# Linear attention times a gated block on one core: the last 64 columns of q made with the last third of k and v, tokens as rows, and turned by PE

## The chip, the cores and the metric

One core of a Trainium2 chip runs the whole kernel as one launch. The time is device microseconds from one execution; a kernel is run several times and the median is compared. The engines named below are PE (matrix products), DVE (vector), ACT (scalar functions), POOL (general) and SP, which here only issues transfers.

## The reference

With x of 2048 tokens by 576 and xn its layer norm:

```
q, k, v = split(xn @ wqkv)            # 32 heads of 18 columns
phi(t)  = where(t > 0, t + 1, exp(t)) + 1e-6
kv      = sum over tokens of phi(k) * v,   z = sum over tokens of phi(k)
o       = phi(q) @ kv / (phi(q) @ z + 1e-6)
s       = o @ wo
g       = silu((gelu(xn @ w_gate) * (xn @ w_up)) @ w_down)     # 4608 columns inside
out     = x + s * g
```

All data are 32-bit floats. The products are made in several passes over a high and a low word of each operand, which are added in PSUM.

## The kernel before

**Stages.** The 2048 tokens are 16 tiles of 128, in 4 blocks of 512. First the layer norm and the tiles of k and v run, then attention (q, kv times wo, the division, s), then gate and up (with seven products where eight would be written plainly, the same for down), then the product down with the closing arithmetic. The change lies in the first two.

**Operands.** 576 is cut in two halves of 288, and each half into 128, 128 and 32 rows (the 32 rows three times, for the mixed passes). `center` scales a tile of x, `turn` (L160) transposes it on PE into two banks of 3 x 128 columns, so that the last 128 columns of each bank are free, `place` (L169) writes the high words (ACT) and low words (DVE) into the blocks' operands `xo`, and `save` (L186) keeps the whole values in `xf` and gives the banks back.

**A tile of k and v.** `kv_tile` (L378) runs three series of matmuls, `x_mm(t, 0)`, `(t, 1)` and `(t, 2)`, each of 2 halves x 7 passes (`KV_PASSES`) over 384 columns of the 1152 columns of k and v, tokens as rows. Behind the first series the next tile is turned, behind the second it is placed and saved, `k_post` makes phi of k (two DVE passes, an exponential on ACT, an addition on POOL), `v_post` copies v on ACT. `kv_mm` adds a tile's phi(k) times v to two banks of their own, a tile later. `end` is a list of further steps, run behind the third series and ahead of `v_post(t, 2)`. The weights stay in five buffers `wkv` of six pieces, the sixth piece of each holding a part of the sixth (third, half).

**q.** `q_mm` (L400) makes one group of 128 rows of q for a block of 512 tokens, q's columns as rows, in 14 matmuls of 512 columns, and `phi` (L300) follows it: the first pass on DVE, or on ACT where its last argument is true. There are five groups: four of 126 columns (seven heads) with two more columns each, and the last, which has 64 columns twice. `q_store` stores the groups of blocks 0 and 1 to memory (they are loaded later by `q_load`), `q_hold` keeps those of blocks 2 and 3. Tiles 0 to 7 come first, then ten groups of `q_store` with a list `behind` of side work, one entry behind each, then tiles 8 to 15, then `q_hold` of block 2 and of block 3, five groups each, with their own lists of side work.

**The side work at the places of the change.** `difference` forms sums of blocks in place (DVE); `form` builds one of them as an operand in buffer 12 and sends it to memory (`keep`), so that the next `form` has to wait until the copy has left; `spread` and `scales` work out the statistics of two tiles (DVE, two short ACT passes). After tile 15: `kv_done` masks kv, `kv_wo` multiplies it with wo, `make_sel` (L532) makes 0/1 matrices on POOL, with copies on ACT and POOL, and the buffer of denominators. `den(tb)` multiplies phi(q) with z, takes reciprocals (DVE) and splits them in two words; `scale` spreads them over the rows of q by a matmul and multiplies; `halve` cuts the result into words; `s_mm` makes s.

**Order and buffers.** `pin` keeps each engine's instructions in the order of the program, so a wait holds up all that stands behind it on that engine, and transfers are issued in order on SP. PSUM has six banks that are shared in turn (`bank`) and two of their own. Four buffers `tmp` hold short-lived values, six buffers `gl` others; a big buffer is named by its number.

Of the kernel before, what the change touches and what calls it, by code (L numbers as in the profile page):

```python
# [15 lines left out]
P = 128  # L16
# [16 lines left out]


Q4 = 64
Q2 = NHG * P // 2
LN_EPS = 1e-5
# [14 lines left out]
@with_exitstack  # L52
def block_kernel(ctx, tc, x, xe, wq_d, wkv_d, wo, wgu_d, wd_d, out):
    nc = tc.nc
# [105 lines left out]
    def turn(n, new=bank):  # L160

        xs = xstat[n // 2][:, n % 2]
        tiles = [new(f"xt_{n}_{j}") for j in range(2)]
        xts[n] = [t[:, 0 : 3 * P].rearrange("p (k t) -> p k t", k=3) for t in tiles]
        for j in range(2):
            for k in range(3):
                pin(nc.tensor.transpose(xts[n][j][:, k, :], xs[:, j, k * P : (k + 1) * P], ident))  # L167
# [64 lines left out]

    TW = 2 * D // 3
    KV = [(c, j) for c in range(3) for j in range(2)]
    wkv = [big(4 + i, [P, 6, TW], F32R, f"wkv_{i}") for i in range(5)]

    def kv_part(c, j, i):
        n = KV.index((c, j))
        return wkv[n][:, i, :] if n < 5 else wkv[i][:, 5, :]

    raws = {}

    def load_kv(c, j):
        n = KV.index((c, j))
        if n % 2 == 0:
            raws["kv", n // 2] = big((2, 3, 12)[n // 2], [P, 2, 3, TW], F32, f"rw_{n}")
        raws[c, j] = raws["kv", n // 2][:, n % 2]
        dma(out=raws[c, j], in_=wkv_d[c, j])

    def kv_hi(c, j):  # L250
        n = KV.index((c, j))
        if n < 5:
            act(wkv[n][:, 0:3, :], raws[c, j], AF.Copy)
        else:
            for i in range(3):
                act(kv_part(c, j, i), raws[c, j][:, i, :], AF.Copy)

    def kv_lo(c, j, eng, mixed=(False, True)):

        n, raw, r = KV.index((c, j)), raws[c, j], slice(2 * KR, 3 * KR)  # L260
        if False in mixed:
            if n < 5:
                eng("tensor_sub", wkv[n][:, 3:5, :], raw[:, 0:2, :], wkv[n][:, 0:2, :].bitcast(F32))
# [60 lines left out]
    KV_PASSES = [(0, 0), (1, 1), (3, 0), (4, 1), (0, 3), (1, 4), (2, 2)]  # L324
    pkv, pks, vas, es = {}, {}, {}, {}
# [28 lines left out]
    def v_post(t, c):  # L354

        if c == 1:
            vas[t] = slot([P, NHG, P], F32, f"va_{t}")
            pool("memset", vas[t][:, :, 0:1], 1.0)
        va, src = vas[t], pkv.pop((t, c))
        n = 2 * TW - D  # L360
        if c == 1:
            src = src[:, TW - n : TW]
            act(va[:, 0, 1 : GW + 1], src[:, 0:GW], AF.Copy)
            act(va[:, 1, 1 : n - GW + 1], src[:, GW:n], AF.Copy)
        else:
            a = 2 * GW - n
            act(va[:, 1, n - GW + 1 : GW + 1], src[:, 0:a], AF.Copy)
            act(
                va[:, 2:4, 1 : GW + 1],
                src[:, a : a + 2 * GW].rearrange("p (g j) -> p g j", g=2), AF.Copy,  # L370
            )
            act(va[:, 4, 1 : W4 + 1], src[:, a + 2 * GW : TW], AF.Copy)

    def run(todo, n=None):
        for _ in range(len(todo) if n is None else min(n, len(todo))):
            todo.pop(0)()

    def kv_tile(t, mid_=(), end=()):  # L378

# [16 lines left out]
        v_post(t, 2)  # L396

    ph, ph_d = {}, {}

    def q_mm(tb, gi, o):  # L400
# [3 lines left out]
        for j, nm in enumerate(BS[b]):  # L404
            for wi, xi, rows in PASSES:
# [4 lines left out]
                n += 1  # L410
        phi(o, pq, f"q{tb}_{gi}", tb == 3)

    def q_store(tb, gi):
        if gi == 0:
            ph_d[tb] = dr.tile([P, NHG, TBN], F32, name=f"phd_{tb}")
        o = gl_tile([P, TBN], f"ph_{tb}_{gi}")
        q_mm(tb, gi, o)
        dma(out=ph_d[tb][:, gi, :], in_=o)

    def q_hold(tb, i, after):  # L420
        ph[tb] = big(i, [P, NHG, TBN], F32, f"ph_{tb}")
        for gi in range(NHG):
            q_mm(tb, gi, ph[tb][:, gi, :])
            run(after[gi])

    def q_load(tb, i):
# [105 lines left out]
    def make_sel():  # L532
# [4 lines left out]
        at["rd"] = rd = buf[:, n : n + TBN]  # L537
        one = tmp([H, NHG, P], "self")
        pool("memset", one, 1.0)
        four, last = one[:, 0:4, 0:GW], one[:, 4, :].rearrange("p (r j) -> p r j", r=2)  # L540
        for o, pattern, base in ((four, [[GW, 4], [1, GW]], 0), (last, [[0, 2], [1, Q4]], 4 * GW)):
# [13 lines left out]
            base=1 - H, pattern=[[0, 4], [0, P - GW]], channel_multiplier=1,  # L555
        )
        for i in range(4):
# [5 lines left out]
        pool("memset", rd.bitcast(F32), 0.0)  # L563

    HB = TBN // 4

    def den(tb):

        pd = bank(f"d_{tb}")
        for gi in range(NHG):  # L570
            for i in range(4):
                mm(
                    pd[H * i : H * (i + 1), 0:HB], at["zc"][:, gi, :],
                    ph[tb][:, gi, i * HB : (i + 1) * HB],
                    start=(gi == 0), stop=(gi == NHG - 1),
                )
# [11 lines left out]
    def scale(tb, *gs):  # L588

        for gi in gs:  # L590
            pb = bank(f"b_{tb}_{gi}")
            mm(pb, at["sel"][:, gi, :], at["rd"], start=True, stop=True)
            p = ph[tb][:, gi, :]
            vec("tensor_mul", p, p, pb)

    def halve(tb, *gs):
# [3 lines left out]
        for gi in gs:  # L600
            p = ph[tb][:, gi, :]
            if gi == NHG - 1:
# [475 lines left out]
    x_mm(1, 2)  # L1078
    save(2)
    v_post(0, 2)  # L1080
    center(3)
    v_post(1, 2)
    make_masks()
# [21 lines left out]
    x_next(4)  # L1105
    v_post(2, 2)
    load_q(0)
    for n in range(3, 2 * TT):
# [21 lines left out]
    def form(nm):  # L1130
# [3 lines left out]
        0: [lambda: kv_mm(N0 - 1), lambda: difference(0, 3)],  # L1134
        1: [lambda: spread(N0, 2)],
        2: [lambda: scales(N0), lambda: center(N0)],
        3: [lambda: form("T1")],
        4: [lambda: turn(N0), lambda: place(N0)],
        5: [lambda: center(N0 + 1)],
        6: [lambda: form("T3"), lambda: save(N0)],  # L1140
        7: [lambda: spread(N0 + 2, 2), lambda: scales(N0 + 2)],
        8: [],
        9: [],
    }
    for i in range(2 * NHG):
        q_store(*divmod(i, NHG))
        run(behind[i])
    for n in range(N0, 2 * N0):
        ends = []
        if n < 2 * N0 - 2:  # L1150
            ends.append(lambda n=n: center(n + 2) if n == N0 else x_next(n + 2))
        if n in (N0, N0 + 2):
            ends.append(lambda n=n: form("T2" if n == N0 else "T4"))
        if n == 2 * N0 - 3:
            ends.append(load_wo)
        if n == 2 * N0 - 1:
            ends += [lambda i=i: difference(1, i) for i in range(3)]
        kv_tile(n, end=ends)
        if n in (N0, N0 + 2):
            load_x(n + 4, 2)  # L1160
    q_hold(2, 7, [
        [lambda: kv_mm(2 * N0 - 1), kv_done, lambda: difference(1, 3)],
        [lambda: kv_wo(4)],
        [lambda: kv_wo(0), lambda: kv_wo(1), move_rows],
        [lambda: kv_wo(2), lambda: kv_wo(3)],
        [make_sel],
    ])
# [116 lines left out]
```

## Time and profile before

| | us |
|---|---|
| median of 3 runs (1503.47 to 1503.78) | 1503.70 |
| the profiled execution, its own time | 1503.52 |
| its span, first to last instruction | 1501.8 |
| DVE busy | 1062.2 |
| ACT busy | 557.1 |
| POOL busy | 534.3 |

The span is what the trace shows; the time has some 1.7 us around it. A line of a group says: line, engine, operation, what it writes and reads, its shape, how often; then the time that it was busy, the mean of one in ns; then how long the engine had stood idle just before, and what ended that. All operations go through helpers, so L84 is any ACT pass, L87 any DVE pass, L90 most matmuls, L93 any POOL operation, L96 any transfer; the tiles' names tell them apart. In the timeline a row is start, length, engine, line, operation and count, with the idle time before it in brackets; several instructions of one kind are one row. A row by stage has the stretch, then busy time and count of PE, PEld, DVE, ACT and POOL, then the granted clock of PE, the busy share of the transfer engines, and GB/s.

### The profile page before, as it was taken

Reading aid. Unit: us, or ns where it says so; the run is one execution under the profiler, and the core shown is the slowest. Engines: PE = TensorE matmul, PEld = TensorE weight load, DVE = VectorE, ACT = ScalarE, POOL = GpSimd, SP = SyncE. Lnnn points to the kernel's source line nnn. Section 1 sums busy time; section 2 is a strip of 40 time slices with the busy share of each in tenths; the row PEclk is TensorE's granted clock in tenths of the full one; section 3 lists DMA queues with packets and bytes.
Section 4 is the critical chain, followed back from the end, with each engine's and each line's share of the span. In section 5 each row is a group of like instructions: output and inputs, shape, how many; then the busy total and the mean of one; then the engine's idle time right before and its main releaser. Section 6 shows DMA issues by size and latency. Waiting matters only on the chain.

```text
span 1501.8 us, 22404 instructions
## 1 busy us (share of the span) xinstructions
PE 1491.9 (99%) x8430; PEld 1335.1 (89%) x8430; DVE 1062.2 (71%) x1583; ACT 557.1 (37%) x1016; POOL 534.3 (36%) x491
## 2 busy tenths in 40 slices
PE   8999999999999999999999999999999999999998
PEld 8989979988888888888888888888899999999998
DVE  7477467467887877887877788877785566555775
ACT  5524345432322323322233232232445454444443
POOL 4342240136555445655544655544410020000120
PEclk9999999999999999999999999999999999999999
DMA  5424104454434233443333443423597766786873
GB/s 194 182 88 147 58 2 182 158 199 170 172 137 163 110 134 144 172 165 142 135 117 130 172 172 135 161 107 134 212 341 246 234 209 230 234 280 228 296 247 116
DMA packets 112215, 257.35 MB, mean 171 GB/s; under 512 B 10138, under 2 KB 38682, under 8 KB 110058
## 3 DMA queue, kind: packets, MB, share of 16 engines
q1 hardware_dynamic: 110474, 247.00, 46.0%
q0 software_dynamic: 1632, 8.91, 1.6%
q8 instruction: 66, 1.08, 0.3%
q14 instruction: 43, 0.35, 0.1%
HBM read 157.93 MB, written 97.91 MB: 170 GB/s over the span
## 4 chain that ended last, share of the span: by engine, by line
PE 96%; DVE 2%; ACT 1%; POOL 0%; DMA 0%; issue 0%; SPq 0%; ACTq 0%; DVEq 0%; POOLq 0%
PE bd L906 27%; PE al L700 15%; PE de L700 15%; PE ga L700 15%; PE be L700 8%; PE kv L90 7%; PE q L90 4%; PE s L90 4%; PE kv_a L90 1%; PE xt L167 1%; DMA rw<-in_wkv_dram 0%; PE b L90 0%; PE kw L90 0%; PE d L90 0%; DVE wkv L87 0%
## 5 line engine op out<-in xcount | busy, mean ns | idle before, releaser
L906 PEld LDWEIGHTS bd<-t,s 128*128 128x128 f32 x3024 | 400.9, 188 | 0.1
L906 PE MATMUL bd<-t,s 128*128 128x288 f32 x3024 | 401.0, 295 | 0.0
L87 DVE TENSOR_TENSOR s<-sr,s 128x512 fp32r<-128x512 f32 x252 | 176.7, 741 | 119.7 <-ACT s L84 115.2
L84 ACT ACTIVATE s<-sr 128x512 fp32r<-128x512 f32 x252 | 149.3, 626 | 189.4 <-PE bd L906 129.0
L93 POOL TENSOR_TENSOR hs<-h,h 128x512 f32<-128x512 f32 x68 | 94.7, 1401 | 205.3 <-DVE h L87 202.6
L84 ACT ACTIVATE h<-h 128x512 f32<-128x512 f32 x108 | 67.0, 632 | 244.4 <-POOL sm L93 123.1
L93 POOL TENSOR_TENSOR sx<-sx 128x288 f32<-128x288 f32 x24 | 28.2, 1195 | 322.6 <-DVE sx L87 211.6
L90 PE MATMUL kv<-wkv,xo_B 128*128 128x384 f32 x672 | 125.2, 340 | 1.7 <-POOL wkv L93 0.9
L90 PEld LDWEIGHTS kv<-wkv,xo_B 128*128 128x128 f32 x672 | 115.9, 188 | 3.9 <-POOL wkv L93 1.7
L87 DVE TENSOR_TENSOR wa<-raw,wa 128x256 fp32r<-128x256 f32 x72 | 79.1, 1099 | 50.1 <-ACT wa L84 46.9
L93 POOL TENSOR_TENSOR sm<-raw 128x384 f32<-128x384 f32 x72 | 75.9, 1054 | 105.9 <-DMA raw<-in_wgu_dram 92.3
L87 DVE TENSOR_TENSOR h<-h,u 128x512 f32<-128x512 f32 x108 | 95.7, 886 | 3.7
L84 ACT ACTIVATE wa<-sm 128x1152 fp32r<-128x1152 f32 x36 | 41.8, 1161 | 136.6 <-PE de L700 136.6
L93 POOL TENSOR_TENSOR td<-td 128x288 f32<-128x288 f32 x72 | 72.2, 1003 | 50.0 <-DMA td<-in_wd_dram 45.8
L87 DVE TENSOR_TENSOR wa<-sm,wa 128x768 fp32r<-128x768 f32 x72 | 63.1, 876 | 36.9 <-ACT wa L84 36.0
L87 DVE TENSOR_TENSOR wb<-raw,wb 128x256 fp32r<-128x256 f32 (+1 forms) x108 | 71.8, 665 | 7.3 <-ACT wb L84 5.8
L87 DVE TENSOR_TENSOR wb<-sm,wb 128x256 fp32r<-128x256 f32 x72 | 61.4, 853 | 20.5 <-ACT wb L84 20.0
L84 ACT ACTIVATE u<-al 128x512 f32<-128x512 f32 x72 | 40.8, 592 | 88.3 <-PE al L700 88.3
L90 PE MATMUL q<-xo_B,wq 128*128 128x512 f32 x240 | 64.1, 395 | 0.0
L87 DVE TENSOR_TENSOR u<-u,ga 128x512 f32<-128x512 f32 x72 | 49.3, 686 | 19.9 <-PE ga L700 19.3
L700 PE MATMUL al<-xo_B,wa 128*128 128x512 f32 x252 | 63.0, 389 | 0.0
L700 PE MATMUL be<-xr_T,wa 128*128 128x512 f32 x252 | 63.0, 389 | 0.0
(159 smaller groups left out, 2783.5 us busy)
## 6 DMA issues: line engine op xcount, KB each, us to landing
sr<-hs SPq DMA_DIRECT2D x252, 256.0 KB
hs<-h SPq DMA_DIRECT2D x68, 512.0 KB
raw<-in_wgu_dram SPq DMA_DIRECT2D x36, 768.0 KB
hs<-hs SPq DMA_DIRECT2D x102, 256.0 KB
td<-in_wd_dram SPq DMA_DIRECT2D x18, 576.0 KB
td<-td SPq DMA_DIRECT2D x18, 576.0 KB
tr<-td SPq DMA_DIRECT2D x16, 576.0 KB
tr<-in_wd_dram SPq DMA_DIRECT2D x12, 576.0 KB
```

The source lines that it names most:

```text
L84: pin(nc.scalar.activation(*args, **kw))
L87: pin(getattr(nc.vector, op)(*args, **kw))
L90: pin(nc.tensor.matmul(*args, **kw))
L93: pin(getattr(nc.gpsimd, op)(*args, **kw))
L167: pin(nc.tensor.transpose(xts[n][j][:, k, :], xs[:, j, k * P : (k + 1) * P], ident))
L700: nc.tensor.matmul(o, w[0:rows, wi, :], xop[0:rows, xi, :], start=(start and n == 0), stop=(n == len(PASSES) - 1), skip_group_check=True,)
L906: nc.tensor.matmul(banks[j][:, 0:HALF], hw[n, s][:, a, t * P : (t + 1) * P], w[:, c, g % 4], start=(new and g == 0 and m == 0), stop=(g == ...
```

## The change

The last group of q (64 columns) is no longer a product of its own. Its 64 columns of the weights are joined to the last third of k and v, so the third series of each tile has 448 columns instead of 384. `q_post` makes phi of those 64 columns with tokens as rows and writes it twice side by side; `q_turn` transposes the 128 x 128 result on PE, into the free last 128 columns of the banks of a later tile's `turn` (tile t's in the turn of tile t + 2); `q_keep`, at the end of `place`, copies it on ACT into a block's buffer `ph4`, which is stored for blocks 0 and 1. The last two tiles are turned in a bank of their own by `last_turn`.

```
 W4 = WIDTHS[4]
...
-Q2 = NHG * P // 2
+Q2 = 2 * P
...
             for k in range(3):
                 pin(nc.tensor.transpose(xts[n][j][:, k, :], xs[:, j, k * P : (k + 1) * P], ident))
+        q_turn([t for t in sorted(pqt) if t < n - 1], [(t, 3) for t in tiles])
...
+        q_keep()
...
     TW = 2 * D // 3
+    CW = [TW, TW, TW + Q4]
...
-                    o[:, 0:TW], xo[s][BS[b][j]][:, xi, i * P : (i + 1) * P], kv_part(c, j, wi),
+                    o[:, 0 : CW[c]], xo[s][BS[b][j]][:, xi, i * P : (i + 1) * P], kv_part(c, j, wi),
...
+    def q_post(t):
+
+        w = tmp([P, 4, Q4], f"w_q{t}")
+        src, o, e = pkv[t, 2][:, TW : CW[2]], w[:, 2], w[:, 3]
+        vec("tensor_scalar", e, src, 0.0, None, op0=ALU.min)
+        vec("tensor_scalar", o, src, 0.0, EPS, op0=ALU.max, op1=ALU.add)
+        act(e, e, AF.Exp)
+        for i in range(2):
+            pool("tensor_add", w[:, i], o, e)
+        pqt[t] = w[:, 0:2]
+
+    def q_turn(ts, banks):
+
+        for t, (b, i) in zip(ts, banks):
+            o = b[:, i * P : (i + 1) * P]
+            pin(nc.tensor.transpose(o, pqt.pop(t), ident))
+            pqx[t] = o
+
+    def q_keep():
+        for t in sorted(pqx):
+            tb, i = divmod(t, TT)
+            if i == 0:
+                ph4[tb] = gl_tile([P, TBN], f"ph4_{tb}")
+                if tb < 2:
+                    ph_d[tb] = dr.tile([P, NHG, TBN], F32, name=f"phd_{tb}")
+            act(ph4[tb][:, i * P : (i + 1) * P], pqx.pop(t), AF.Copy)
+            if i == TT - 1 and tb < 2:
+                dma(out=ph_d[tb][:, 4, :], in_=ph4[tb])
...
-    def kv_tile(t, mid_=(), end=()):
+    def kv_tile(t, mid_=(), end=(), after=()):
...
         v_post(t, 2)
+        q_post(t)
+        run(list(after))
...
-        phi(o, pq, f"q{tb}_{gi}", tb == 3)
+        phi(o, pq, f"q{tb}_{gi}", tb % 2 == 1)
...
-        for gi in range(NHG):
+        for gi in range(4):
             q_mm(tb, gi, ph[tb][:, gi, :])
```

In the first two tiles, which are written out by hand, `q_post(0)` stands behind `save(2)` and `q_post(1)` behind `center(3)`. The side work is dealt out again, since eight groups of `q_store` are left of ten, and four of five in each `q_hold`:

```
     behind = {
         0: [lambda: kv_mm(N0 - 1), lambda: difference(0, 3)],
-        1: [lambda: spread(N0, 2)],
-        2: [lambda: scales(N0), lambda: center(N0)],
-        3: [lambda: form("T1")],
+        1: [lambda: spread(N0, 2), lambda: scales(N0)],
+        2: [lambda: center(N0), lambda: form("T1")],
+        3: [lambda: spread(N0 + 2, 2), lambda: scales(N0 + 2)],
         4: [lambda: turn(N0), lambda: place(N0)],
-        5: [lambda: center(N0 + 1)],
-        6: [lambda: form("T3"), lambda: save(N0)],
-        7: [lambda: spread(N0 + 2, 2), lambda: scales(N0 + 2)],
-        8: [],
-        9: [],
+        5: [lambda: center(N0 + 1), lambda: form("T3")],
+        6: [lambda: save(N0)],
+        7: [],
     }
-    for i in range(2 * NHG):
-        q_store(*divmod(i, NHG))
+    for i in range(8):
+        q_store(*divmod(i, 4))
...
-        if n in (N0, N0 + 2):
-            ends.append(lambda n=n: form("T2" if n == N0 else "T4"))
+        after = [lambda n=n: form("T2" if n == N0 else "T4")] if n in (N0, N0 + 2) else []
...
+        if n == 2 * N0 - 2:
+            after.append(make_sel)
         if n == 2 * N0 - 1:
+            after.append(copy_sel)
             ends += [lambda i=i: difference(1, i) for i in range(3)]
-        kv_tile(n, end=ends)
+        kv_tile(n, end=ends, after=after)
...
     q_hold(2, 7, [
-        [lambda: kv_mm(2 * N0 - 1), kv_done, lambda: difference(1, 3)],
+        [lambda: kv_mm(2 * N0 - 1), kv_done, last_turn, lambda: difference(1, 3)],
         [lambda: kv_wo(4)],
         [lambda: kv_wo(0), lambda: kv_wo(1), move_rows],
         [lambda: kv_wo(2), lambda: kv_wo(3)],
-        [make_sel],
     ])
     q_hold(3, 8, [
         [lambda: den(2)],
-        [],
         [lambda: scale(2, 0, 1), lambda: halve(2, 0, 1)],
         [lambda: scale(2, 2, 3), lambda: halve(2, 2, 3)],
         [lambda: scale(2, 4), lambda: halve(2, 4)],
```

`copy_sel` is the last part of `make_sel`, its four copies of the 0/1 matrices; the rest of `make_sel` now runs a tile earlier. The weights reach the kernel as three arrays of k and v instead of one, and q's array has 512 columns instead of 640, so `prep_q` works on pieces of 256 columns instead of 320. In `q_hold(3)` one group now stands between `den(2)` and the first `scale`, where there were two.

More of the change, by code (lines that the diff above doesn't have):

```diff
@@ L52, in block_kernel @@
 @with_exitstack
-def block_kernel(ctx, tc, x, xe, wq_d, wkv_d, wo, wgu_d, wd_d, out):
+def block_kernel(ctx, tc, x, xe, wq_d, wkv0_d, wkv1_d, wkv2_d, wo, wgu_d, wd_d, out):
     nc = tc.nc
@@ L233, in block_kernel, with kv_parts @@
     TW = 2 * D // 3
+    CW = [TW, TW, TW + Q4]
     KV = [(c, j) for c in range(3) for j in range(2)]
-    wkv = [big(4 + i, [P, 6, TW], F32R, f"wkv_{i}") for i in range(5)]
+    wkv_d = [wkv0_d, wkv1_d, wkv2_d]
+    wkv = [big(4 + i, [P, 5 * CW[KV[i][0]] + CW[2]], F32R, f"wkv_{i}") for i in range(5)]
+    def kv_parts(n, i0, i1):
+        w = CW[KV[n][0]]
+        return wkv[n][:, i0 * w : i1 * w].rearrange("p (i f) -> p i f", f=w)
     def kv_part(c, j, i):
         n = KV.index((c, j))
-        return wkv[n][:, i, :] if n < 5 else wkv[i][:, 5, :]
+        if n < 5:
+            return kv_parts(n, i, i + 1)[:, 0]
+        w = 5 * CW[KV[i][0]]
+        return wkv[i][:, w : w + CW[2]]
     raws = {}
@@ L245, in load_kv @@
         if n % 2 == 0:
-            raws["kv", n // 2] = big((2, 3, 12)[n // 2], [P, 2, 3, TW], F32, f"rw_{n}")
+            raws["kv", n // 2] = big((2, 3, 12)[n // 2], [P, 2, 3, CW[c]], F32, f"rw_{n}")
         raws[c, j] = raws["kv", n // 2][:, n % 2]
-        dma(out=raws[c, j], in_=wkv_d[c, j])
+        dma(out=raws[c, j], in_=wkv_d[c][j])
     def kv_hi(c, j):
@@ L252, in kv_hi @@
         if n < 5:
-            act(wkv[n][:, 0:3, :], raws[c, j], AF.Copy)
+            act(kv_parts(n, 0, 3), raws[c, j], AF.Copy)
         else:
@@ L262, in kv_lo @@
             if n < 5:
-                eng("tensor_sub", wkv[n][:, 3:5, :], raw[:, 0:2, :], wkv[n][:, 0:2, :].bitcast(F32))
+                eng("tensor_sub", kv_parts(n, 3, 5), raw[:, 0:2, :], kv_parts(n, 0, 2).bitcast(F32))
             else:
@@ L324, in block_kernel @@
     KV_PASSES = [(0, 0), (1, 1), (3, 0), (4, 1), (0, 3), (1, 4), (2, 2)]
-    pkv, pks, vas, es = {}, {}, {}, {}
+    pkv, pks, vas, es, pqt, pqx, ph4, ph, ph_d = ({} for _ in range(9))
     def x_mm(t, c):
@@ L358, in v_post @@
             pool("memset", vas[t][:, :, 0:1], 1.0)
-        va, src = vas[t], pkv.pop((t, c))
+        va, src = vas[t], pkv[t, c]
         n = 2 * TW - D
@@ L396, in kv_tile @@
         v_post(t, 2)
-    ph, ph_d = {}, {}
+        q_post(t)
+        run(list(after))
     def q_mm(tb, gi, o):
@@ L420, in q_hold, with ph_of @@
     def q_hold(tb, i, after):
-        ph[tb] = big(i, [P, NHG, TBN], F32, f"ph_{tb}")
-        for gi in range(NHG):
+        ph[tb] = big(i, [P, 4, TBN], F32, f"ph_{tb}")
+        for gi in range(4):
             q_mm(tb, gi, ph[tb][:, gi, :])
             run(after[gi])
+    def ph_of(tb, gi):
+        return ph4[tb] if gi == 4 and tb > 1 else ph[tb][:, gi, :]
     def q_load(tb, i):
@@ L537, in make_sel @@
         at["rd"] = rd = buf[:, n : n + TBN]
-        one = tmp([H, NHG, P], "self")
+        at["one"] = one = tmp([H, NHG, P], "self")
         pool("memset", one, 1.0)
@@ L556, in make_sel, with copy_sel @@
         )
+        pool("memset", rd.bitcast(F32), 0.0)
+    def copy_sel():
+        one, sel = at["one"], at["sel"]
         for i in range(4):
@@ L592, in scale @@
             mm(pb, at["sel"][:, gi, :], at["rd"], start=True, stop=True)
-            p = ph[tb][:, gi, :]
+            p = ph_of(tb, gi)
             vec("tensor_mul", p, p, pb)
@@ L600, in halve @@
         for gi in gs:
-            p = ph[tb][:, gi, :]
+            p = ph_of(tb, gi)
             if gi == NHG - 1:
@@ L1079, in block_kernel @@
     save(2)
+    q_post(0)
     v_post(0, 2)
     center(3)
+    q_post(1)
     v_post(1, 2)
@@ L1106, in block_kernel @@
     v_post(2, 2)
+    q_post(2)
     load_q(0)
@@ L1251 @@
     xe = np.concatenate([xh] + 3 * [xh[:, :, 2 * P :]], axis=2)
-    wq = np.zeros((D, NHG, P), A_wqkv.dtype)
-    for g in range(4):
-        wq[:, g, 0:GW] = A_wqkv[:, g * GW : (g + 1) * GW]
-        wq[:, g, GW:P] = A_wqkv[:, 4 * GW + Q4 + 2 * g : 4 * GW + Q4 + 2 * g + 2]
-    wq[:, 4, 0:Q4] = wq[:, 4, Q4:P] = A_wqkv[:, 4 * GW : 4 * GW + Q4]
-    wq = halves(wq.reshape(D, NHG * P)).reshape(2, P, 3, 2, Q2).transpose(3, 0, 1, 2, 4)
-    wkv = halves(A_wqkv[:, D:]).reshape(2, P, 3, 3, 2 * D // 3).transpose(3, 0, 1, 2, 4)
+    q, n = A_wqkv[:, 0:D], 2 * D // 3
+    last = q[:, 4 * GW : 4 * GW + Q4]
+    wq = np.concatenate([
+        q[:, i : i + w] for g in range(4)
+        for i, w in ((g * GW, GW), (4 * GW + Q4 + 2 * g, 2))
+    ], axis=1)
+    wq = halves(wq).reshape(2, P, 3, 2, Q2).transpose(3, 0, 1, 2, 4)
+    wkv = [halves(A_wqkv[:, D + c * n : D + (c + 1) * n]) for c in range(2)]
+    wkv.append(halves(np.concatenate([A_wqkv[:, D + 2 * n :], last], axis=1)))
     wgu = np.stack([
@@ L1269 @@
     for name, a in (
-        ("x", xs), ("xe", xe), ("wq", wq), ("wkv", wkv), ("wo", A_wo), ("wgu", wgu), ("wd", wd)
+        ("x", xs), ("xe", xe), ("wq", wq), ("wkv0", wkv[0]),
+        ("wkv1", wkv[1]), ("wkv2", wkv[2]), ("wo", A_wo), ("wgu", wgu), ("wd", wd)
     ):
```

9 lines of the change are left out of this document (5 added, 4 removed).

## The prediction

> **What bounds the kernel now.** I read the page first, then the chain of waits, then the busy time by stage, then PE's own waits, then the timeline at each place that the change touches.
>
> ```profile
> span 1501.8 us, 22404 instructions
> ...
> PE 1491.9 (99%) x8430; PEld 1335.1 (89%) x8430; DVE 1062.2 (71%) x1583; ACT 557.1 (37%) x1016; POOL 534.3 (36%) x491
> ...
> PEclk9999999999999999999999999999999999999999
> ...
> PE 96%; DVE 2%; ACT 1%; POOL 0%; DMA 0%; issue 0%; SPq 0%; ACTq 0%; DVEq 0%; POOLq 0%
> ```
>
> PE is busy at the full granted clock and carries 96% of the chain that ends last, so a matmul taken away is worth its time unless a wait replaces it. The change lies in the first 232 us. Cut at its stages (columns: stretch, length, then busy time of PE, PEld, DVE, ACT, POOL):
>
> ```profile
> 0.00:32.45 32.45, 28.00 (x155) 24.96 (x156) 23.80 (x56) 17.52 (x40) 15.15 (x25) 1.00 0.48 182
> 32.45:82.94 50.49, 50.49 (x324) 50.36 (x323) 26.08 (x69) 22.98 (x64) 19.84 (x23) 1.00 0.45 165
> 82.94:116.54 33.60, 33.60 (x157) 27.99 (x157) 28.13 (x50) 10.43 (x18) 12.45 (x10) 1.00 0.35 141
> 116.54:187.19 70.65, 70.65 (x450) 70.42 (x449) 40.48 (x96) 30.19 (x84) 17.84 (x23) 1.00 0.25 86
> 187.19:209.25 22.06, 22.06 (x103) 17.86 (x101) 17.86 (x31) 7.35 (x18) 6.07 (x7) 1.00 0.01 3
> 209.25:232.42 23.17, 22.65 (x147) 18.51 (x149) 13.29 (x23) 12.44 (x23) 12.15 (x15) 1.00 0.00 1
> ```
>
> These are the start, the tiles of k and v, the first q stage (ten groups), the later tiles, the third token block's q with kv times wo, and the last block's q. PE is full in all but the start and the last stage. DVE has 5.5 us to spare in the first q stage (28.13 of 33.60) and 4.2 in the fifth. PE's waits before 330 us confirm that little is lost:
>
> ```profile
> PE kv L90 <- POOL wkv L93: 0.9, 1, 0.9
> PE b L90 <- DVE aux L87: 0.6, 2, 0.5
> PE kv L90 <- ACT xo_B L84: 0.5, 2, 0.3
> ```
>
> **The change, part by part.** The pace of a matmul is not its mean duration, since neighbours overlap; I take it from runs of them in the chain (start, length, count):
>
> ```profile
> 41.49 4.88 PE kv L90 x28
> ...
> 87.19 12.78 PE q L90 x56
> 99.97 0.66 PE xt L167 x6
> ...
> 277.82 18.65 PE s L90 x140
> ```
>
> Removed: group 4 of q for four token blocks, 4 x 14 = 56 matmuls of 512 columns. The row of q is exactly 56 of them: **-12.78 us**.
>
> Widened: the last third of k and v goes from 384 to 448 columns, in 16 tiles x 14 = 224 matmuls. No row has 448 columns. The paces are 18.65/140 = 0.1332 us at 288, 4.88/28 = 0.1743 at 384, 12.78/56 = 0.2282 at 512: 0.43 and 0.42 ns a column, so 64 columns cost 0.0270 to 0.0274 us and all 224 cost 6.04 to 6.14. The outer bounds are nothing (384's pace) and 12.1 (512's); the three widths lie on a line, so I take **+6.10**.
>
> Added on PE: 16 transposes of 128 x 128, the same operation as in the row of six: 0.66/6 = 0.11 us each, **+1.76**. They write the free last quarter of banks that are held already, and but for the last two they stand behind six others.
>
> ```profile
> L167 PE MATMUL xt<-ident,x 128*128 128x128 f32 x96 | 13.2, 273 | 0.9 <-PE idle L1021 0.8
> ```
>
> This row has 273 ns as the duration of one. [...] Here six take 0.66 us together, so the measurement decides for 0.11 unless they stand alone.
>
> The side work of each tile: two DVE passes of 128x64 from PSUM, one exponential, two POOL adds and one ACT copy of 128x128.
>
> ```profile
> L87 DVE TENSOR_SCALAR e_k<-kv 128x384 f32<-128x384 f32 x16 | 8.9, 558 | 39.3 <-PE kv L90 39.3
> ...
> L87 DVE TENSOR_SCALAR e_k<-kv 128x192 f32<-128x192 f32 x16 | 5.7, 357 | 10.0 <-PE kv L90 9.9
> ...
> L84 ACT ACTIVATE va<-kv 128x60 f32<-128x60 f32 x16 | 3.5, 221 | 9.4 <-PE kv L90 9.4
> L93 POOL TENSOR_TENSOR wq_l<-rq,wq 128x320 fp32r<-128x320 f32 x4 | 3.5, 878 | 0.0
> ```
>
> From 192 and 384 columns a 64-column DVE pass is an estimated 0.22 us (bounds 0 and 0.36); the exponential 0.22; a POOL add 0.3 (bounds 0 and 0.88). Per tile that is 0.44 on DVE, some 0.5 on ACT, 0.6 on POOL, beside DVE 40.48, ACT 30.19 and POOL 17.84 busy of 70.65 us: hidden, if the columns are ready when PE turns them. The turn stands in PE's queue before the next tile's second matmul series, so everything on PE waits for a late add. The worst ordinary tile is one where statistics run on DVE first:
>
> ```profile
> 56.87 0.68 DVE L87 TENSOR_SCALAR x<-x,mv,st 128x768 f32<-128x768 f32 x1
> ```
>
> and in the chain of waits
>
> ```profile
> 58.95 0.65 PE xt L167 x6
> ```
>
> DVE is free at 57.55, so its passes end at 58.0, the exponential at 58.2, the adds at 58.8 (60.0 at their bound). PE reaches the turn at 58.95 + 0.65 + 0.38 (the wider series before it, 6.10/16) = 60.0. Cost nothing; without that cover, each microsecond of lateness costs one, in up to 14 tiles. The extra store of 256 KB per early block goes onto SP once a block, ahead of loads that are wanted tiles later: nothing.
>
> The start: two pieces of the weights are a sixth wider on the last third, so one ACT pass, one DVE pass, POOL's three and a 32-row piece grow, and two tiles' q work comes in.
>
> ```profile
> L84 ACT ACTIVATE wkv<-rw 128x1152 fp32r<-128x1152 f32 x5 | 5.7, 1159 | 0.3 <-DMA rw<-in_wkv_dram 0.3
> ...
> L87 DVE TENSOR_TENSOR wkv<-rw,wkv 128x768 fp32r<-128x768 f32 x3 | 2.9, 954 | 0.0
> ```
>
> ```profile
> 12.00:14.00 2.00, 1.69 (x10) 0.89 (x8) 1.70 (x3) 1.63 (x4) 1.17 (x2) 1.00 1.03 418
> ```
>
> ACT +0.19 and DVE +0.16 by a sixth, four DVE passes 0.9, and 197 KB more at 418 GB/s (the last figure of the stage row, transfers full) 0.5 us. PE comes 0.76 us later itself through two wider series (counted above), which hides most: bounds 0 and 1.8, all in a row; I take **+0.3**, the growth of the two passes ahead of that series.
>
> The last turn: tokens of tiles 14 and 15 are turned behind the first q group of block 2 and kv's last products. Tile 15's DVE passes wait behind three differences.
>
> ```profile
> 184.44 6.44 DVE L87 TENSOR_TENSOR xf_B<-xf_B,xf_B 128x1536 f32<-128x1536 f32 x3
> ...
> 191.15 0.29 PE L90 MATMUL kv_b<-pk,va 128*73 128x72 f32 x2
> ```
>
> DVE 190.88 + 0.44, ACT 0.22, POOL 0.6: 192.15. PE is there at 191.44 + 0.38 = 191.82. Stall 0.3, bounds 0 and 1.5 (adds at 0.88); nearer the first, **+0.4**. Behind it wait block 2's other groups; DVE and ACT have slack there.
>
> The last q stage loses two groups of 3.2 us, under which masks were made and denominators worked out.
>
> ```profile
> 212.29 1.30 PE L90 MATMUL d<-ph,small 128*32 128x128 f32 x40
> ...
> 214.75 1.48 ACT L84 ACTIVATE aux<-self 32x640 fp32r<-32x640 f32 x2 [4.10 <-POOL self L93]
> ...
> 217.50 0.28 DVE L87 TENSOR_SCALAR r<-d 128x128 f32<-128x128 f32 x1
> ...
> 219.20 1.28 DVE L87 TENSOR_TENSOR aux<-r,aux 32x128 fp32r<-32x128 f32 x4 [0.44 <-ACT aux L84]
> ...
> 220.63 0.70 PE L90 MATMUL b<-aux 128*128 128x512 f32 x2 [0.47 <-DVE aux L87]
> ```
>
> Before, the products d end at 213.6, but the reciprocals begin at 217.5, since ACT stands 4.1 us at the mask copies that POOL delays, and DVE behind ACT. The reciprocal chain itself takes 220.48 - 217.50 = 3.0 us. With the masks made a tile earlier it can begin when d ends, and one group of 3.2 us covers it instead of two. The wait of 0.47 should go; the spacing of scaling and group after that is as before. I take **-0.4**, bounds -0.75 (with the 0.28 of the next row, before the last products of s) and +3.2 (a rival).
>
> ```profile
> 231.63 0.56 PEld L90 LDWEIGHTS s<-kv,pq 128*128 128x128 f32 x4 [0.28 <-DVE pq L87]
> ```
>
> The first q stage loses 6.4 us of PE cover as well, and DVE two groups' passes, and the first pass of block 1's four groups goes to ACT.
>
> ```profile
> L87 DVE TENSOR_SCALAR e_q<-q 128x512 f32<-128x512 f32 x15 | 10.3, 687 | 3.6 <-PE q L90 3.5
> ```
>
> By the stage's row DVE needs 28.13 - 8 passes of 0.69 = 22.6 of 27.4 us (33.60 - 6.4 + 0.22): as full as before, so nothing; if it runs over, PE's six banks hold some three groups of backlog.
>
> **Sum:** -12.78 + 6.10 + 1.76 + 0.3 + 0.4 - 0.4 = **-4.6 us**. The span goes from 1501.8 to 1497.2. The profiled execution took 1503.52 us, 1.7 around its span: 1498.9. The median of the runs is 0.18 above it, so **1499.1**.
>
> **Rivals.**
> *The last q stage is DVE's and ACT's.* From d to the first scaling before took 7 us, and half the cover goes. For it: the chain of waits there runs through ACT and DVE. Against: 4.1 us of that was the masks. Price: that one group's cover, 3.2 us: 1502.3.
>
> *Transposes count singly,* 273 ns by the row above: 16 x 0.163 = 2.6 more, 1501.7. [...] For it: two stand alone at the end. Against: 0.66 for six.
>
> *The gain doesn't arrive*, because 448 columns are paced like 512: 6.0 more, 1505.1. Against it: three widths on a line. Break-even is (12.78 - 1.76)/224 = 0.0492 us per matmul above the 384 pace; the line gives 0.0272.
>
> *Slower: the copies of the sums in the first q stage.* One buffer serves both T1 and T3, so the second's build on ACT waits until the first has left for memory.
>
> ```profile
> 101.90 0.32 SPq L96 DMA_DIRECT2D kept_T<-xo_T  x1
> ...
> 108.40 1.47 ACT L84 ACTIVATE xo_T<-xf_B 128x1536 fp32r<-128x1536 f32 x1
> 109.90 1.92 DVE L87 TENSOR_TENSOR xo_T<-xf_B,xo_T 128x1024 fp32r<-128x1024 f32 x2 [1.48 <-ACT xo_T L84]
> ...
> 111.92 0.49 ACT L84 ACTIVATE xf_B<-xt 128x384 f32<-128x384 f32 x1 [1.67 <-DVE xo_T L87]
> ```
>
> From the build to the save that frees the two transpose banks it takes 4 us (108.40 to 112.41), and tile 9's turn needs those banks. PE gets there 6.2 us earlier than now, near 112.5. The copy now leaves at most 6.5 us before the build and was no wait. After, it is issued near 100 and the build stands at 105 to 107: no stall up to a landing at 108.5, and slower than before from a landing past 113, twice the time. At 13.5: 5 us, 1504.1; with phi's ACT passes queued behind it, which block 1 now has twice, up to 1507.
>
> **How the numbers follow.** Two runs of this kernel can't tell 0.2% (3.0 us) from no change. Chances: the sum 0.74 (own range 1497.6 to 1500.6, from the bounds of start, last turn and last stage); last q stage 0.08; single transposes 0.04; no gain through the width 0.04; slower through the copies 0.10, most of it past 0.2%. Faster by over 0.2% is the first, 0.74; within 0.2% the next three and a fifth of the last, 0.18; slower 0.08. The range reaches from 1497.6 to 1502.3 and leaves out the last two cases.
>
> **What would show it.** Right: 224 matmuls of q where there were 280; the third series of a tile at 0.201 us each (14 in 2.82); eight transposes in 0.88; no PE wait over 0.5 us between 82 and 125; the reciprocals starting within a microsecond of d. Wrong: a wait of PE for a POOL add or an ACT copy at the turns in many tiles; a wait at tile 9's turn; PE idle before b or s over 1 us.

## The result and the profile after

The changed kernel takes 1501.04 us, median of 19 runs (1500.76 to 1501.5), where the kernel before took 1503.69 beside it (19 runs). The ratio is 0.9981, 95% interval [0.9974, 0.9988]: faster, by 2.65 us or 0.18%, just under the 0.2% that the prediction gave as its bound for a difference. The profiled execution took 1501.39 us around its span of 1499.7.

The page of the changed kernel has PE as full as before, with 40 matmul instructions less (56 of q gone, 16 transposes new):

```profile
span 1499.7 us, 22460 instructions
...
PE 1489.9 (99%) x8390; PEld 1330.9 (89%) x8390; DVE 1063.7 (71%) x1604; ACT 562.1 (37%) x1047; POOL 537.2 (36%) x519
```

So the question is where along PE's chain the time went. The groups by shape, before 330 us, confirm what was removed and added (192 + 32 = 224 products of q, 224 of 448 columns), and the side work came close to its estimates of 0.22 us for a DVE pass, 0.22 for the exponential and 0.3 for a POOL add:

```profile
L91 PE MATMUL q<-xo_B,wq 128*128 128x512 f32 x192 | 52.0, 397 | 0.0
L91 PE MATMUL kv<-wkv,xo_B 128*128 128x448 f32 x224 | 48.9, 368 | 0.1
...
L91 PE MATMUL q<-xo_B,wq_l 128*128 128x512 f32 x32 | 12.5, 390 | 0.0
L94 POOL TENSOR_TENSOR w_q<-w_q 128x64 f32<-128x64 f32 x32 | 9.6, 320 | 24.6 <-ACT w_q L85 24.6
...
L88 DVE TENSOR_SCALAR w_q<-kv 128x64 f32<-128x64 f32 x32 | 5.6, 218 | 16.6 <-ACT va L85 16.6
L85 ACT ACTIVATE w_q<-w_q 128x64 f32<-128x64 f32 x16 | 4.2, 261 | 14.1 <-DVE w_q L88 14.1
```

The chain of waits of the changed kernel gives the stages (start, length, what, how many):

```profile
35.18 5.34 PE kv L91 x28
...
44.80 5.34 PE kv L91 x28
...
54.41 5.34 PE kv L91 x28
...
88.81 3.27 PE q L91 x14
...
116.17 2.45 PE kv L91 x14
...
191.17 3.27 PE q L91 x14
...
195.45 0.44 PE q_last L402 x2
...
228.96 0.79 PE s L91 x4
...
293.81 3.20 PE al L746 x14
```

Held against the same points of the kernel before, whose first gate product starts at 296.47, and against the prediction's terms dealt to the stages (d, the products for the denominators, is taken from the two timelines: 212.29 before, 213.50 after):

| stage | before, us | after, us | forecast | measured |
|---|---|---|---|---|
| start, to tile 2's double series | 32.45 | 35.18 | 0.76 + 0.22 + 0.3 = +1.28 | +2.73 |
| tiles 2 to 7 | 50.49 | 53.63 | 6 x 0.381 + 4 x 0.11 = +2.73 | +3.14 |
| first q stage | 33.60 | 27.36 | -6.39 + 0.11 = -6.28 | -6.24 |
| tiles 8 to 15 | 70.65 | 75.00 | 8 x 0.381 + 7 x 0.11 = +3.82 | +4.35 |
| third block's q, to d | 25.10 | 22.33 | -3.20 + 0.22 + 0.4 = -2.58 | -2.77 |
| d to the last products of s of block 2 | 19.34 | 15.46 | -3.20 - 0.4 = -3.60 | -3.88 |
| from there to the first gate product | 64.84 | 64.85 | 0 | +0.01 |
| sum | | | -4.63 | -2.66 |

Up to the first gate product the changed kernel gains 2.66 us. The start costs 1.45 us more than forecast, the tiles 0.94 more, and the rest comes out 0.42 better. The median of the runs gains 2.65, but the span of the profiled execution only 2.1 (1499.7 for 1501.8): it lost about 0.5 us much later, at the start of the product down, where PE waited for DVE, which the profile of the kernel before doesn't show there:

```profile
PEld bd L952 <- DVE u L88: 0.5, 1, 0.5
```

So the stages account for the difference of the medians, and the 0.35 us by which this execution stands above the median lies outside the change.

**The start.** Two things went wrong there. The timeline of the kernel before comes first and then that of the changed one (start, length, engine, with idle time and its releaser in brackets); `wkv<-rw,wkv` makes the low words of a piece of the weights of k and v.

```profile
19.07 1.52 DVE L87 TENSOR_TENSOR wkv<-rw,wkv 128x768 fp32r<-128x768 f32 x2
...
20.07 3.46 POOL L93 TENSOR_TENSOR wkv<-rw,wkv 128x384 fp32r<-128x384 f32 x3 [3.54 <-ACT wkv L84]
...
23.59 0.23 POOL L444 MEMSET ones<- 128x160 f32 x1
```

```profile
8.89 0.55 DVE L88 TENSOR_TENSOR wkv<-rw,wkv 32x384 fp32r<-32x384 f32 x1
...
13.35 3.25 POOL L94 TENSOR_TENSOR wkv<-rw,wkv 128x768 fp32r<-128x768 f32 x2 [1.14 <-ACT wkv L85]
...
15.67 1.34 DVE L88 TENSOR_TENSOR wkv<-rw,wkv 32x384 fp32r<-32x384 f32 x1
...
19.14 2.69 DVE L88 TENSOR_TENSOR wkv<-rw,wkv 128x896 fp32r<-128x896 f32 x2
...
20.19 3.88 POOL L94 TENSOR_TENSOR wkv<-rw,wkv 128x448 fp32r<-128x448 f32 x3 [3.60 <-ACT wkv L85]
...
32.01 0.23 POOL L487 MEMSET ones<- 128x160 f32 x1
...
33.52 0.58 POOL L94 TENSOR_TENSOR w_q<-w_q 128x64 f32<-128x64 f32 x2
...
34.16 0.33 PE L402 MATMUL xt<-ident,w_q 128*128 128x128 f32 x1 [0.41 <-POOL w_q L94]
```

First, DVE's two passes over the fifth piece (last third, first half), 128 rows and then 32, took 1.52 us and now take 2.69, where a sixth more work would make 1.8. The view of this tile has each pass, before and after (count, then shortest, median and longest in ns, and the starts):

```profile
L87 DVE TENSOR_TENSOR wkv<-rw,wkv x2: 550/754/959, 19.1 to 20.0; 128x768 fp32r<-128x768 f32 x1, 32x384 fp32r<-32x384 f32 x1
```

```profile
L88 DVE TENSOR_TENSOR wkv<-rw,wkv x2: 1093/1337/1581, 19.1 to 20.2; 128x896 fp32r<-128x896 f32 x1, 32x448 fp32r<-32x448 f32 x1
```

Before, the 32 rows (0.55 us) began at 20.05, a moment ahead of POOL's own piece at 20.07. Now the first pass is wider, POOL starts at 20.19, 0.04 us before that pass ends, and the 32 rows take 1.58 us beside POOL. It happens elsewhere in this trace too: the 32-row pass takes 0.55 us at 8.89, where POOL is idle as it begins, and 1.34 at 15.67, beside POOL's pieces. The Trainium skill (SBUF — State Buffer, "Who interferes with whom") says that a vector instruction with two inputs in SBUF contends with a GpSimd instruction that reads SBUF, that the lock is exclusive, and that the order of issue decides which one is held up; 0.55 against 1.34 agrees. DVE comes 1.2 us later to phi of k, and with it PE to tile 0's wider series (23.01 for 21.78). The run with an unused buffer further below, which has the whole change, names that wait of PE, 1.3 us where the kernel before had 0.2:

```profile
PE kv L91 <- DVE pk L88: 1.3, 1, 1.3
```

In the changed kernel's own profile it doesn't show, because PE ran at a lower granted clock just before and came later by itself (last section).

Second, `make_masks` takes its row of ones from the four temporary buffers that are used in turn, and the new q work of tiles 0 and 1 now takes from them too. So the masks slid from 23.6 to 32.0 on POOL and stand right ahead of the first additions of q (33.52), for which PE waits at the turn. PE's waits before 330 us name it, in the first row here:

```profile
PE xt L402 <- POOL w_q L94: 0.8, 2, 0.4
...
PE b L91 <- DVE aux L88: 0.2, 1, 0.2
```

**The tiles.** A double series (14 matmuls of 448 and 14 of 384) takes 5.34 us where two of 384 took 4.88: 0.46 a tile where the line through three widths gave 0.381. Over 14 tiles that is 1.1 us more than forecast; the transposes, at 0.10 to 0.11 us each, give a little back.

### The profile page after: what moved, and what is told of

It reads as the page before. It is cut to its first block, busy times and chain, and to the rows that moved or that the text cites. A ratio compares the mean times of both kernels' runs of the same rounds, so it can differ in the third digit from the quotient of the medians.

```text
span 1499.7 us, 22460 instructions
## 1 busy us (share of the span) xinstructions
PE 1489.9 (99%) x8390; PEld 1330.9 (89%) x8390; DVE 1063.7 (71%) x1604; ACT 562.1 (37%) x1047; POOL 537.2 (36%) x519
## 4 chain that ended last, share of the span: by engine, by line
PE 97%; DVE 1%; DMA 0%; POOL 0%; ACT 0%; issue 0%; SPq 0%; POOLq 0%; ACTq 0%
PE bd L952 26%; PE al L746 15%; PE de L746 15%; PE ga L746 15%; PE kv L91 8%; PE be L746 8%; PE s L91 4%; PE q L91 3%; PE kv_a L91 1%; PE xt L168 1%; DMA tr<-in_wd_dram 0%; PE idle L1067 0%; PE d L91 0%; PE kw L91 0%; PE b L91 0%
## 5 line engine op out<-in xcount | busy, mean ns | idle before, releaser
L91 PE MATMUL kv<-wkv,xo_B 128*128 128x384 f32 (+1 forms) x672 | 133.3, 353 | 1.3 <-POOL wkv L94 0.9
L91 PEld LDWEIGHTS kv<-wkv,xo_B 128*128 128x128 f32 x672 | 120.0, 190 | 6.8 <-POOL wkv L94 1.6
L746 PE MATMUL al<-xr_B,wa 128*128 128x512 f32 x252 | 63.0, 389 | 0.0
L746 PE MATMUL be<-xo_T,wa 128*128 128x512 f32 x252 | 63.0, 389 | 0.0
```

Of the source, the lines that this page charges most:

```text
L91: pin(nc.tensor.matmul(*args, **kw))
L746: nc.tensor.matmul(o, w[0:rows, wi, :], xop[0:rows, xi, :], start=(start and n == 0), stop=(n == len(PASSES) - 1), skip_group_check=True,)
```

## The experiments

All are edits of the changed kernel, and all ratios are against the kernel before, run on the same chip. Its median beside them was 1503.66 to 1503.73 us, so times are also compared with the changed kernel's 1501.04.

**The masks at the start, first try.** The ones get a buffer of their own.

```diff
-        ones = tmp([P, NHG * H], "ones")
+        ones = sb.tile([P, NHG * H], F32, name="ones")
```

> The changed kernel (1501.0 us), but the row of ones from which the masks are cut has a buffer of its own instead of one of the four short-lived ones. Theory A: in the changed kernel the masks had to wait for a short-lived buffer, ran on POOL at 32 to 34 us ahead of the first q additions, and held PE at the turn of tile 3 for 1.0 us: now they run before 5 us, that wait goes, 1500.0 us. Rival: the start is late through its own longer chain on DVE and ACT, the turn's wait only takes the place of a wait for the place step behind it: 1501.0 within 0.2.

Measured: 1501.87 us, ratio 0.9988 [0.9979, 0.9997], later than both numbers expected. The start did gain: no wait at the turn is left, tile 2's double series begins at 33.95 instead of 35.18, the first gate product at 292.38 instead of 293.81. But the gate and up stage took 802.09 us, from there to the first product down at 1094.47; before it took 799.70 (296.47 to 1096.17). The groups of this run between 300 and 1080 us show two of its products slower than all the others, which take 389 ns in the mean here and in the changed kernel:

```profile
L746 PE MATMUL al<-xr_B,wa 128*128 128x512 f32 x245 | 62.6, 394 | 0.0
L746 PE MATMUL be<-xo_T,wa 128*128 128x512 f32 x245 | 62.1, 392 | 0.0
...
L746 PE MATMUL al<-xo_B,wa 128*128 128x512 f32 x245 | 61.2, 389 | 0.0
```

62.6 and 62.1 against 61.2 make 2.3 of the 2.4 us. So the late masks did hold the start, and the edit has a second effect hundreds of microseconds later. Two causes are possible, the new buffer (which can move others) and the masks' new place in time; they are told apart further below.

**The third series at its old width.** The tile's third series computes 384 columns again, and q's passes read v's columns: the last 64 columns of q are not computed.

```diff
-                    o[:, 0 : CW[c]], xo[s][BS[b][j]][:, xi, i * P : (i + 1) * P], kv_part(c, j, wi),
+                    o[:, 0:TW], xo[s][BS[b][j]][:, xi, i * P : (i + 1) * P], kv_part(c, j, wi)[:, 0:TW],
...
-        src, o, e = pkv[t, 2][:, TW : CW[2]], w[:, 2], w[:, 3]
+        src, o, e = pkv[t, 2][:, 0:Q4], w[:, 2], w[:, 3]
```

> The changed kernel, with the third series back at 384 columns; the q passes read 64 of v's columns instead, so the last 64 columns of q are not computed, while every other instruction stays. Theory A: a matmul of 448 columns costs 0.207 us against 0.1735, so 224 x 0.0335 = 7.5 us go: 1493.5. Rival (the line through 288, 384 and 512 columns holds, the loss is elsewhere): 6.1 us go, 1494.9.

Measured: 1495.23 us, ratio 0.9944 [0.9931, 0.9956]; 5.8 us below the changed kernel. Its chain has the old double series back:

```profile
35.27 4.86 PE kv L91 x28
```

(5.34 - 4.88) x 14 tiles = 6.4 us is the price of the width in tiles 2 to 15. The first two tiles' narrower series brought nothing, since tile 2 starts where it did (35.27): the start is held by DVE and POOL, not by PE. PE waits 0.4 us more at the first turns and 0.5 at the last one, which the wide series had covered. So the total lies nearer to the rival's 6.1 us, but the pace in the tiles is theory A's; the total alone would have misled.

**No transposes.** The first 14 turns of q are left out.

```diff
+            if i == 3:
+                pqt.pop(t)
+                pqx[t] = b[:, 0:P]
+                continue
```

> The changed kernel without 14 of the 16 transposes of q (the last two stay); the copies behind them read a transposed piece of x instead, so the last 64 columns of q are not made for 14 tiles. Theory A: 14 x 0.11 = 1.5 us and the 1.0 us that the turn of tile 3 waits for POOL: 1498.5. If a transpose counts with the 0.27 us that its row shows: 14 x 0.27 + 1.0 = 4.8, 1496.2. If the transposes hide and the wait is replaced: 1501.0.

Measured: 1499.1 us, ratio 0.9968 [0.9956, 0.9981]; 1.9 us less, where 2.5 was expected. The chain of this run gives the period of a tile as 53.05 - 43.54 = 9.51 us, against 54.41 - 44.80 = 9.61:

```profile
43.54 5.34 PE kv L91 x28
...
53.05 5.34 PE kv L91 x28
```

A transpose costs 0.10 us. The rival of 273 ns each, for which 1496.2 was expected, is refuted. Tile 2 starts at 34.06 here, 1.12 us earlier, since the wait at the first turns is gone, and the first gate product at 291.39, 2.42 earlier, which is close to the 2.5. The profile loses about 0.7 us again at the start of the product down, where PE waits for DVE.

**The selectors in their old place.** `make_sel` and `copy_sel` go back behind the last group.

```diff
-        if n == 2 * N0 - 2:
-            after.append(make_sel)
...
-            after.append(copy_sel)
...
-        [lambda: kv_wo(2), lambda: kv_wo(3)],
+        [lambda: kv_wo(2), lambda: kv_wo(3), make_sel, copy_sel],
```

> The changed kernel with the 0/1 matrices made where they were before, behind the last group of block 2, instead of behind tiles 14 and 15. Theory A (the earlier masks are what let the last q stage lose two groups without a wait): POOL works at them until some 3 us after that group, ACT stands at its copies, the reciprocals begin 1.5 to 2 us later than in the changed kernel, and PE waits that long before the first scaling: 1502.5 to 1503. Rival: one group and the products d cover them: 1501.0.

Measured: 1502.9 us, ratio 0.9995 [0.9986, 1.0004]; 1.86 more. PE's waits (1.9 us for DVE's aux, 0.2 in the changed kernel) and the timeline of this run:

```profile
PE b L91 <- DVE aux L88: 1.9, 2, 1.8
```

```profile
213.91 1.30 PE L91 MATMUL d<-ph,small 128*32 128x128 f32 x40
...
217.24 0.28 DVE L88 TENSOR_SCALAR r<-d 128x128 f32<-128x128 f32 x1
...
220.37 0.70 PE L91 MATMUL b<-aux 128*128 128x512 f32 x2 [1.75 <-DVE aux L88]
```

Reciprocals begin at 217.24 here, 2 us after d ends. In the changed kernel's timeline they begin 0.1 us after d ends (213.50 + 1.30 = 214.80):

```profile
213.50 1.30 PE L91 MATMUL d<-ph,small 128*32 128x128 f32 x40
...
214.90 0.28 DVE L88 TENSOR_SCALAR r<-d 128x128 f32<-128x128 f32 x1
```

So the early selectors (the 0/1 matrices) are what lets one q group cover the denominators; without them the change would be worth 0.8 us.

**The masks at the start, second try.** The ones lie in a part of `small` that is free then; no buffer moves.

```diff
-        ones = tmp([P, NHG * H], "ones")
+        ones = small[:, 448:608]
```

> The changed kernel with the row of ones in columns 448 to 607 of the buffer of masks, which nothing else uses: the masks run early as in e1, and no other buffer is moved. Theory A: start 1.2 us earlier and every matmul later as in the changed kernel, 1499.8 us. If the loss of e1 in the gate and up stage came from the masks' new place in time and not from moved buffers: 1501.9 again.

Measured: 1499.69 us, ratio 0.9968 [0.9956, 0.9979]. The chain of this run:

```profile
34.06 5.34 PE kv L91 x28
...
292.70 3.20 PE al L746 x14
```

Tile 2 begins 1.12 us earlier, the first gate product 1.11, and gate and up takes its old 799.70 us (down starts at 1092.40). So the late masks cost 1.1 us of span, and the loss in the first try came with the new buffer and not from the masks' place in time.

**The 32 rows first.** DVE does its short pass ahead of POOL's piece.

```diff
-    kv_lo(2, 0, vec)
+    kv_lo(2, 0, vec, (True,))
+    kv_lo(2, 0, vec, (False,))
```

> The changed kernel with DVE's 32-row pass over the weights of the last third ahead of its 128-row pass instead of behind it. Theory A: in the changed kernel the first pass ends some 40 ns after POOL has begun its own, and the second, of 0.5 us, then takes 1.58 because the two engines don't work on such operands at once; in the other order the short pass is over before POOL begins, DVE reaches phi of k 1.0 us earlier, and all that follows moves with it: 1500.0 us. Rival (the pass is slow by its width and rows alone, or POOL then delays the third series instead): 1501.0.

Measured: 1500.64 us, ratio 0.9978 [0.9969, 0.9987]; 0.4 less, where 1.0 was expected. The timeline of this run:

```profile
19.22 1.72 DVE L88 TENSOR_TENSOR wkv<-rw,wkv 32x448 fp32r<-32x448 f32 x2
...
20.17 4.12 POOL L94 TENSOR_TENSOR wkv<-rw,wkv 128x448 fp32r<-128x448 f32 x3 [3.60 <-ACT wkv L85]
...
23.31 1.40 DVE L88 TENSOR_SCALAR x<-x,mv,st 128x768 f32<-128x768 f32 x1
```

The two passes take 1.72 us instead of 2.69 (the short one 0.62 and the long one 1.09), so the order was the cause. But DVE's scaling of tile 2 now falls beside POOL's piece and takes 1.40 us where it took 0.68, and PE's wait for POOL at the first turns grows from 0.8 to 1.2 us: with the masks still late, most of the gain waits there.

**A buffer that nobody uses,** allocated early and filled once, to see if any shift of the buffers slows gate and up.

```diff
+    spare = sb.tile([P, NHG * H], F32, name="spare")
+    nc.gpsimd.memset(spare, 1.0)
```

> The changed kernel with one unused buffer of 640 bytes a partition, filled once at the start, ahead of the big buffers; nothing else is changed. If moved buffers alone slow some matmuls of gate and up, as e1 seems to show, the same products (the first with x's second block set and the second) are paced at 0.230 to 0.234 us instead of 0.227 and the time is 2.4 us longer: 1503.4. If not: 1501.0.

Measured: 1500.73 us, ratio 0.998 [0.9971, 0.9989]: no slowdown, and all products of gate and up at 389 ns. That any added buffer does it falls. It depends on where the buffer stands, and why these two products of the first try slow down stays open.

**The pace by width.** Fourteen groups of 14 matmuls each behind tile 13, of 320 to 512 columns, every group into a bank of its own.

```diff
+        for k, (w, a) in enumerate(WS):
+            o = bank("t" + "abcdefghijklmnop"[k])
+            for i in range(14):
+                mm(
+                    o[:, 0:w], xo[1]["B11"][:, i % 3, (i % 4) * P : (i % 4 + 1) * P],
+                    wkv[4][:, a + (i % 4) * 512 : a + (i % 4) * 512 + w],
...
+    WS = [(320, 0), (384, 0), (400, 0), (416, 0), (432, 0), (440, 0), (448, 0), (448, 64),
+          (456, 0), (464, 0), (480, 0), (496, 0), (512, 0), (408, 0)]
```

> The changed kernel with 14 groups of 14 matmuls behind tile 13, each group of one width (320, 384, 400, 416, 432, 440, 448, 448 from a start 64 columns on, 456, 464, 480, 496, 512, 408 columns), same operands as the third series, results unused; only their pace is read. If 448 columns cost 0.207 us by their number alone, the paces show it here too, with 384 at 0.1735 and 512 at 0.227, and the steps between say where it comes from. If the pace of 0.207 comes from what else goes on during a tile (PSUM reads, other engines), 448 stands on the line, at 0.200.

Measured, in one execution of 1539.44 us, in the chain of waits (tb is 384 wide, tg 448, tm 512):

```profile
174.79 2.43 PE tb L91 x14
...
187.93 2.84 PE tg L91 x14
...
205.59 3.19 PE tm L91 x14
```

The middle of 2.43 and 3.19 is 2.81, and 448 takes 2.84: a little above the line, but less than in the tile, where 5.34 - 2.43 leaves 2.91. Neither expectation holds as it stands.

**The pace by operands.** Eight groups of 14 in the same place with the tile's own series and parts of the operands of the run before exchanged: ta and th as in the tile, tb and tc 384 wide, td to tg 448 wide with other stationary or moving operands.

```diff
+        series("ta", 448, 2)
+        series("tb", 384, 2)
+        series("tc", 384, 0)
+        series("td", 448, 2, weight=turning)
+        series("te", 448, 2, moving=near)
+        series("tf", 448, 2, moving=far)
+        series("tg", 448, 2, weight=turning, moving=far)
+        series("th", 448, 2)
```

> The changed kernel with eight groups of 14 matmuls behind tile 13, results unused, only the pace is read: the third series as it stands (448 columns), the same at 384, the first series at 384, then the third series with the stationary operands in the order of e5, with its moving operand from the pieces of one buffer 448 apart, from starts 512 apart as in e5, with both as in e5, and as it stands again. If 0.207 us belongs to the operands as they lie, the first and last groups show 0.207, the group with both as in e5 shows 0.203, and the two between say which operand it is. If it belongs to the tile's other work, all groups of 448 show 0.203.

Measured, in one execution of 1523.49 us, in the chain of waits:

```profile
172.97 2.93 PE ta L91 x14
175.90 2.43 PE tb L91 x14
...
180.76 2.89 PE td L91 x14
...
192.33 2.89 PE th L91 x14
```

Six groups of 448 take 2.89 or 2.93 away from a tile's own series, 0.2064 us a matmul for 2.89. (2.89 - 2.43) x 14 tiles = 6.4 us, which is what the tiles lost: the pace belongs to these matmuls of this width, not to what else a tile does. No exchange of operands brought back the 2.84 of the run before, not even the one meant to repeat it (tg, 2.89); what gives 2.84 there stays open (its stationary operands came from one buffer, here from two).

**Both edits of the start,** the ones in `small` and the 32 rows first.

> The changed kernel with both repairs of the start, the row of ones in free columns of the masks' buffer (e6) and DVE's short pass first (e7). Theory A: the masks no longer stand ahead of the q additions, so the third of a microsecond or so that e7's shorter DVE chain leaves after the scaling of tile 2 waits for POOL reaches PE: 1499.2 to 1499.4 us, against 1499.7 for e6 alone. Rival (PE's own wider series set the start once the masks are away): 1499.7.

Measured: 1499.23 us (1499.06 to 1499.48, 6 runs), ratio 0.9967 [0.9955, 0.9979]. In its chain the double series of tile 2 begins at 33.66, the earliest of all with the change whole, and the first gate product at 292.25. This version beats both kernels: 1.8 us below the changed one and 4.5 below the one before. The start is 1.21 us longer than before (33.66 for 32.45; 0.78 counted from the scaling of tile 1, which came 0.43 us later in this execution), not more than the 1.28 that the prediction's terms gave: these two effects are what it missed there.

## Why the prediction was right or wrong

The direction, the mechanism and the range (1497.6 to 1502.3) held, but the range held partly by luck. The time of 1499.1 was 1.9 us too low, and 1501.04 lies 0.4 above the 1497.6 to 1500.6 that the likeliest case had for itself. It lies in the part that was added for rivals, and these proved false. By the stated bound of 0.2% the gain counts as no difference, which had 0.18, not as faster, which had 0.74; the bound was coarser than the measurement, whose interval is 0.14% wide.

- **Removed, -12.78.** Right: the three stages with fewer groups lost 12.89 us where 12.46 was forecast with the small terms, and 224 products of q are left.
- **Widened, +6.10.** Mis-sized. That the three widths lie on a line was taken to hold at a fourth between them. Measured in the tiles 0.46 each where 0.381 was forecast, 6.4 over 14 tiles for 5.3; the runs at 448 alone and at 384 again show it. The stated sign of 2.82 us for 14 came out at 2.89 to 2.93. The first two tiles' share did not count in the changed kernel, whose start is held by DVE and POOL.
- **Transposes, +1.76.** Right: 0.10 each for 0.11 where they stand behind the six others. The rival of 273 ns falls.
- **The start, +0.3.** Mis-sized: the stage grew by 2.73 us where this term with the first tiles' PE work gave 1.28, and the term itself came out at its upper bound of 1.8 (2.73 - 0.98 = 1.75). The step summed longer passes as if each engine ran alone. It missed two things: that POOL's piece would start between two DVE passes (2.69 us for 1.52), and that the masks need a temporary buffer that the new q work holds (1.1 us). With both taken away the kernel won 1.8 us.
- **The tiles' side work at nothing.** Right from the third turn on: no wait for it is in PE's list. At the first two it failed, through the masks.
- **The last turn, +0.4, and the last q stage, -0.4.** Somewhat better than forecast: 0.44 us for two transposes, no wait named, so 0.2 of stall at most; the reciprocals start 0.1 us after d, and the stage gains 3.88 for 3.60. The rival that DVE and ACT bound it is false as the change stands, but it is what happens once the selectors go back (+1.86).
- **First q stage, nothing.** Right, and with it falls the rival that made the change slower: no PE wait stands between 82 and 125 us.
- **The rival that 448 is paced like 512** is false: 2.84 to 2.93 against 3.19 for 14. But the measured pace lies on its side of the line.

## What to carry to other kernels

When a change puts new work into the start of a kernel, follow the temporary buffers and not just the engines: who takes the next of the buffers that are used in turn, and what slides behind it. Where two engines run on the same kind of pass in turn, a few tens of nanoseconds can decide which goes first (0.04 us here), and putting the shorter pass ahead can pay (1.72 us for the two instead of 2.69). A pace at a new width is worth measuring at that width when 200 matmuls hang on it.

## What the hardware showed that was not expected

- The pace of a series steps off the line between 384 and 512 columns: 2.43, 2.84 to 2.93 at 448, 3.19 us for 14.
- One buffer of 640 bytes a partition, added with the masks, made two products of gate and up slower for the whole stage (394 and 392 ns for 389; 2.4 us in all); another one, added earlier, did not. The cause was not found.
- In the changed kernel's profile the granted clock of PE fell to 0.50 for one stretch of the start. The windows show it (PEclk is the third number from the end):

```profile
14.00:16.00 2.00, 2.00 (x7) 1.86 (x7) 1.75 (x5) 1.79 (x3) 1.92 (x2) 0.50 0.91 331
```

It cost nothing: tile 0's wider series starts 10.73 us after the scaling of tile 1 (23.01 - 12.28), and 10.75 us after it in the run with the unused buffer (23.23 - 12.48), whose clock stayed at 1.00. There PE waits 1.3 us for DVE at that place; here the slower matmuls filled the wait. The run by operands shows the same fall to 0.50, the others don't.
